# A fused attention and gated MLP kernel whose hand-ordered step list is reordered behind chunk 0's first layer

## The chip, the core and the metric

The kernel runs on one core of a Trainium2 chip. Engines: TensorE (PE, with its weight loads PEld), VectorE (DVE), ScalarE (ACT), GpSimd (POOL), and SyncE (SP), which here issues DMAs only. The metric is the device time of one execution in microseconds (us); lower is better.

## The reference: what is computed

```python
# q, k, v: [8 batches, 8 heads, 576 tokens, 64]; w_in: [512, 2048]; w_out: [2048, 512]
# causal attention within a sliding window of 64 tokens
scores = q @ k^T, masked to 0 <= i - j < window
x = softmax(scores) @ v                 # -> [4608 tokens, 512]
h = x @ w_in                            # [4608, 2048]
g = h - tanh(h)
out = g @ w_out                         # [4608, 512]
```

## The kernel before, in words

The kernel is a sequence of steps that a person or a search wrote out beforehand. `PLAN` (L536 and following) is a string of words; `play` splits it, and each word calls one function of the table `STEPS` with its numbers (`H.2.5` is `first_layer(2, 5)`; a letter p, a, v or s at the end names the engine: GpSimd, ScalarE, VectorE or SyncE). Each engine and each DMA queue takes its instructions in the order in which the words stand; across engines, semaphores make a step wait for the steps it needs. Nothing reorders it afterwards, so the order of words is the order on every queue.

The MLP works on 9 chunks of 512 tokens (c = 0 to 8):
- `H.c.m` is one of 16 first-layer products of a chunk, four matmuls of 128x512 into one PSUM bank (L431); `Hp.c.m.h` is half of one (L508). Banks: m modulo 2 for c over 1, (m + c) modulo 3 before.
- `A.c.m` takes the tanh of it on ScalarE (L439), `G.c.m` subtracts on VectorE and writes gT (L445); that frees the bank for the next `H`.
- `W.c.s.part` is a quarter of a second-layer product for 128 tokens, four matmuls (L474; L467 for the last block), in bank 2 (chunk 0: 2 and 0; chunk 8: 0 and 2). `O.c.s.eng` copies the sum to ysb, of which there are three buffers (L90 on ScalarE, L92 on VectorE), and SyncE sends it out (L495).

The attention works on pairs of heads g (batch g // 4). For batches up to 2:
- `lk`, `lq` load k and q rows, `ck`, `cq` cast them to bf16; `Fp`, `Ep` transpose them on TensorE (L260) into the bank given as last number, `Fc`, `Ec` copy them out; `Rp` makes the scores (L286), `Rx` their exp (L318).

For batches 3 to 7:
- `lr`, `qr` load k and q rows on GpSimd (L166); `tk`, `tq` transpose them by DMA, issued on SyncE (L171 and L179); `tz` copies the tail of q into q8; `S` makes the scores (L299, L304), `Sx` their exp (L314).

For all pairs:
- `M` multiplies by the 0/1 mask (L323). The mask itself lies in PSUM, in columns 448 to 511 of bank 7. `PP` multiplies with v (L348, banks 5 to 7), `DR` takes the reciprocal of the row sums (L356), `DN` divides (L365, L368), and `Xp`/`Xc` on TensorE (L397) or `Y` by DMA (L416) transposes the result into the x of the MLP.
- `LV` loads v rows on GpSimd (L145), and `Z.b` copies the rows that two tiles share from one half of the partitions to the other, two VectorE copies (L151, L152); in batch 1 `za` and `zb` do this per pair on an engine that is named.
- `wo` loads a part of w_out (L198). `mk` clears two tiles of k by memset on VectorE (L222).

The code that plays the list:

```python
    def play(script):
        for word in script.split():
            what, *args = word.split(".")
            STEPS[what](*[ENG[a] if a in ENG else int(a) for a in args])
```

## Time and profile before

| | |
|---|---|
| time of three runs | 307.33, 307.46, 308.23 us (median 307.46) |
| span of the profiled execution, first to last instruction | 305.2 us |
| the profiled execution's own time | not listed; the median of the runs is 2.26 us longer than its span |
| PE, DVE, ACT, POOL busy | 297.8, 176.2, 157.5, 103.7 us |
| bytes moved by DMA | 36.77 MB, 120 GB/s on average |

In the lines below, a timeline row has the start in us, the busy time in us, engine, line, operation, tiles out<-in, shapes and a count; in brackets stands how long the engine was idle before it and which instruction ended that. Overlapping matmuls are grouped into one row. A groups row of the page has the busy total and the mean in ns of one instruction.

### The profile page before, as it was taken

The numbers are of one execution on the slowest core, as the hardware profiler recorded it, in microseconds if no ns is written. First come the engines' busy times: TensorE is split into PE (matmuls) and PEld (weight loads), VectorE is DVE, ScalarE is ACT, GpSimd is POOL, SyncE is SP. The second block draws the span as 40 slices with busy tenths as digits, with TensorE's granted clock in tenths as the row PEclk, the third lists the DMA queues.
The fourth block names the chain that finished last, engine by engine and source line by source line (L and its number), as shares of the span: only waits on it lengthen the run. The fifth ranks groups of instructions, "written<-read, shape, count | busy, mean of one in ns | idle before, by whom it ended". The sixth has DMA issues, their size and how long they took to land.

```text
span 305.2 us, 6469 instructions
## 1 busy us (share of the span) xinstructions
PE 297.8 (98%) x2599; PEld 149.4 (49%) x2632; DVE 176.2 (58%) x316; ACT 157.5 (52%) x265; POOL 103.7 (34%) x141
## 2 busy tenths in 40 slices
...
PEclk9999999999999999999999999999999999999999
...
GB/s 155 159 195 193 195 207 180 159 205 102 102 143 127 173 125 181 182 108 131 164 177 127 135 173 142 95 143 35 37 76 74 0 69 37 34 34 37 52 51 104
DMA packets 132878, 36.77 MB, mean 120 GB/s; under 512 B 119920, under 2 KB 127344, under 8 KB 132848
## 3 DMA queue, kind: packets, MB, share of 16 engines
...
q8 instruction: 20, 0.33, 0.5%
q14 instruction: 10, 0.08, 0.1%
HBM read 36.70 MB, written 9.44 MB: 151 GB/s over the span
## 4 chain that ended last, share of the span: by engine, by line
PE 87%; DVE 5%; ACT 3%; issue 2%; POOL 2%; DVEq 0%; ACTq 0%; POOLq 0%
PE ps L474 38%; PE ps L431 30%; PE ps L508 6%; PE ps L348 3%; PE ps L304 2%; DVE gT L445 2%; PE ps L397 1%; ACT th L439 1%; PE ps L286 1%; PE ps L467 1%; DVE pt L323 1%; PE ps L260 1%; PE ps L281 1%; PE ps L227 1%; POOL qall L110 1%
## 5 line engine op out<-in xcount | busy, mean ns | idle before, releaser
L445 DVE TENSOR_TENSOR gT<-ps,th 128x512 bf16<-128x512 f32 x144 | 97.2, 687 | 85.3 <-ACT th L439 84.6
L474 PE MATMUL ps<-w_out_sb,gT 128*128 128x512 bf16 x527 | 131.5, 380 | 2.2 <-issue 0.8
L439 ACT ACTIVATE th<-ps 128x512 f32<-128x512 f32 x144 | 84.7, 599 | 93.0 <-PE ps L431 79.7
L431 PE MATMUL ps<-xT,wi 128*128 128x512 bf16 x496 | 120.7, 380 | 0.1
L474 PEld LDWEIGHTS <-gT 128*128 128x128 bf16 x560 | 53.3, 98 | 61.4
L431 PEld LDWEIGHTS <-wi 128*128 128x128 bf16 x496 | 47.0, 98 | 54.3
L145 POOL DMA_DIRECT2D vw<-in_v_dram x35 | 30.0, 872 | 36.1 <-PE ps L348 33.5
L90 ACT ACTIVATE ysb<-ps 128x512 f32<-128x512 f32 (+1 forms) x24 | 14.2, 593 | 30.9 <-PE ps L474 30.2
L166 POOL DMA_DIRECT2D qall<-in_q_dram x25 | 21.7, 881 | 24.1 <-DMA qw<-qall 21.4
L166 POOL DMA_DIRECT2D kall<-in_k_dram x25 | 21.7, 875 | 10.4 <-DMA kw<-kall 4.8
L314 ACT ACTIVATE pt<-ps 128x1024 bf16<-128x1024 f32 (+1 forms) x30 | 23.3, 816 | 3.5 <-PE ps L304 3.2
L323 DVE TENSOR_TENSOR pt<-pt,ps 128x1152 bf16<-128x1152 bf16 x28 | 20.5, 749 | 5.1 <-ACT pt L314 3.2
L508 PE MATMUL ps<-xT,wi 128*128 128x512 bf16 x80 | 20.8, 380 | 0.0
L92 DVE COPY ysb<-ps 128x512 f32<-128x512 f32 (+1 forms) x11 | 7.1, 650 | 20.5 <-PE ps L467 13.2
L368 DVE TENSOR_TENSOR xs<-ps,rcp 128x384 bf16<-128x384 f32 x28 | 15.2, 550 | 0.3
L318 ACT ACTIVATE pt<-ps 128x640 bf16<-128x640 f32 (+1 forms) x24 | 14.7, 659 | 0.8 <-PE ps L286 0.8
L348 PEld LDWEIGHTS <-pt 128*64 128x64 bf16 x504 | 9.4, 112 | 6.3 <-DVE pt L323 2.1
L90 ACT ACTIVATE kt<-ps 128x576 bf16<-128x576 bf16 x10 | 6.5, 647 | 10.8 <-PE ps L256 6.8
L227 PE MATMUL ps<-warm 128*128 128x512 bf16 (+1 forms) x35 | 10.6, 435 | 1.1 <-DVE warm L207 1.1
L508 PEld LDWEIGHTS <-wi 128*128 128x128 bf16 x80 | 7.4, 98 | 8.5 <-issue 0.4
L348 PE MATMUL ps<-vw,pt 128*64 128x65 bf16 x504 | 11.0, 197 | 0.3 <-DVE pt L323 0.2
L365 DVE TENSOR_TENSOR xs<-ps,rcp 128x384 bf16<-128x384 f32 x14 | 7.7, 550 | 0.1
...
## 6 DMA issues: line engine op xcount, KB each, us to landing
...
```

The costliest lines, as they stand in the source:

```text
L90: nc.scalar.activation(o, i, ACT.Copy)
L145: nc.gpsimd.dma_start(out=w[:, 2 * i + 1, :, 0:D] if i < NF else w[64:128, 2 * i, :, 0:D], in_=v[b, :, 128 * i:128 * i + n].rearrange("h p ...
L166: nc.gpsimd.dma_start(out=token_rows(b, n)[0:c, i], in_=(q if n == "q" else k)[b, :, 128 * i:128 * i + c].rearrange("h p d -> p h d"))
L314: nc.scalar.activation(o, sp, ACT.Exp, scale=scale)
L323: nc.vector.tensor_tensor(p, p, mask.unsqueeze(1).to_broadcast([128, 2 * NJ, 64]), ALU.mult)
L348: nc.tensor.matmul(ps[r, bank, 65 * i:65 * i + 65], PT[(g + r2) % NPT][:, j, r], vw[b % 2][:, j, p0 + r2 + NP * h, :], start=True, stop=True)
L368: nc.vector.tensor_tensor(xs[b % 2][:, p0 // 2, 0:6, n // 2, :], ov[:, :, 0:D], sums[g][:, n].to_broadcast([128, 6, D]), ALU.mult)
L431: nc.tensor.matmul(hp, w_in_tile(ki, m), chunk_tile(c)[:, n.start // 64:n.stop // 64, ki % 2, 64 * (ki // 2):64 * (ki // 2) + 64], start=( ...
L439: nc.scalar.activation(th[:, n], hp, ACT.Tanh)
L445: nc.vector.tensor_tensor(gT[c][:, m, columns(s)], hp, th, ALU.subtract)
L474: nc.tensor.matmul(yp, gT[c][:, m, s * 128:(s + 1) * 128], w_out_sb[:, m, :], start=n == 1 and i == 0, stop=n == 4 and i == 3)
L508: nc.tensor.matmul(hp, w_in_tile(half + 2 * i, m), chunk_tile(c)[:, :, half, 64 * i:64 * i + 64], start=n == 1 and i == 0, stop=n == 2 and ...
```

## The change

Only the string `PLAN` changes. Up to `cq.8.v G.0.9 G.0.10 Rp.7.1.3 A.0.11 wo.2 Fc.8.7.a G.0.11 Rp.7.0.5 H.0.12 lk.9.p Rx.7.0.5 A.0.12` (about 36 us into the span) it is the same word by word; behind that the same steps stand in another order to the end. A few steps take another engine (some casts and copies `c`, `Xc`, `O`, `tz`) or another bank for a transpose or a score (`Ep.8` takes bank 7 in place of 1, `Ep.9` bank 1 in place of 7). The number of TensorE instructions is the same. In the new order GpSimd's loads and SyncE's transposes stand in batches of about ten, and `wo` is loaded in the order 2, 1, 3 in place of 2, 3, 1.

The first lines, and those around the places that the prediction speaks of:

```diff
-        cq.8.v G.0.9 G.0.10 Rp.7.1.3 A.0.11 wo.2 Fc.8.7.a G.0.11 Rp.7.0.5 H.0.12 lk.9.p Rx.7.0.5 A.0.12 Ep.8.1
-        Rx.7.1.3 cq.9.v H.0.14 M.4 wo.3 zb.1.3.p G.0.12 Ec.8.1.a PP.4 wo.1 A.0.14 H.0.15 mk DR.4 DN.4.1 G.0.14
-        A.0.15 H.0.13 DN.4.0 za.1.3.a W.0.0.0 Rp.8.0.3 G.0.15 A.0.13 Rp.8.1.5 DN.4.2 zb.1.2.a za.1.2.v Rx.8.1.5
-        W.0.1.0 M.7 qr.3.3 LV.2.3 lk.11.p PP.6 Rx.8.0.3 Xp.1.0.1.3 W.0.0.2 G.0.13 Xp.1.0.0.4 DR.6 Xc.1.0.1.3.a
...
-        A.1.3 Rx.10.1.3 H.1.4 A.1.4 G.1.3 Ec.11.6.a H.1.5 A.1.5 qr.3.0 Z.2 H.1.6 qr.3.2 PP.8 G.1.5 Rp.11.0.3
...
-        G.2.2 H.2.5 Sx.12.2 Sx.12.0 W.1.1.1 Z.3 W.1.1.0 A.2.5 Sx.12.1 O.1.1.a tk.4.1 tq.4.0 M.12 tk.4.0 H.2.4
-        M.13 tk.4.3 tq.4.4 G.2.5 A.2.4 PP.12 W.1.2.3 H.2.7 lr.6.4 lr.5.4 DR.12 DN.12.2 G.2.4 tq.4.3 tk.4.2
...
+        cq.8.v G.0.9 G.0.10 Rp.7.1.3 A.0.11 wo.2 Fc.8.7.a G.0.11 Rp.7.0.5 H.0.12 lk.9.p Rx.7.0.5 A.0.12 Ep.8.7
+        Rx.7.1.3 cq.9.v H.0.14 M.4 wo.1 H.0.13 Ec.8.7.a M.7 G.0.12 A.0.14 PP.4 Rp.8.1.3 H.0.15 A.0.13 Rx.8.1.3
+        G.0.14 DR.4 G.0.13 DN.4.2 DN.4.0 DN.4.1 Rp.8.0.3 zb.1.3.a wo.3 za.1.3.p zb.1.2.p Rx.8.0.3 A.0.15
+        za.1.2.v Ep.9.1 W.0.0.0 Xp.1.0.0.3 Xp.1.0.1.4 Xc.1.0.1.4.a Xc.1.0.0.3.a Ec.9.1.a ck.9.a G.0.15 PP.6
...
+        qr.4.1 LV.3.0 A.1.1 ck.10.v M.8 W.0.3.3 Fp.11.4 Fc.11.4.a Ep.10.6 Ec.10.6.a W.0.3.2 O.0.3.a A.1.3
+        Ec.11.5.v G.1.1 mk Z.2 G.1.3 H.1.4 Hp.1.2.0 Hp.1.2.1 A.1.4 A.1.2 Fp.10.3 Rp.11.0.5 Rp.11.1.4 Rx.11.0.5
+        Fc.10.3.a H.1.6 tk.3.1 tk.3.4 tq.3.4 tk.3.3 tq.3.0 tq.4.4 tq.3.2 tk.3.2 tq.3.3 tq.3.1 tk.3.0 G.1.2 G.1.4
+        M.9 H.1.5 A.1.6 Rx.11.1.4 H.1.7 PP.8 G.1.6 A.1.5 A.1.7 G.1.5 DR.8 DN.8.1 DN.8.2 H.1.9 H.1.8 A.1.9 G.1.7
+        G.1.9 A.1.8 DN.8.0 G.1.8 Rp.10.1.3 Rp.10.0.6 H.1.10 H.1.12 Rx.10.1.3 Rx.10.0.6 A.1.10 M.10 M.11 G.1.10
+        H.1.11 Xp.2.0.1.4 A.1.11 A.1.12 PP.10 H.1.13 G.1.11 A.1.13 tz.3.a DR.10 G.1.12 DN.10.0 G.1.13 DN.10.1
...
+        O.1.0.a Hp.2.1.1 Hp.2.1.0 W.1.1.3 W.1.1.1 A.2.1 A.2.0 lr.5.3 qr.4.2 LV.3.1 LV.4.0 lr.4.0 lr.4.1 lr.4.3
+        LV.3.4 lr.5.2 LV.4.2 qr.5.4 lr.4.4 qr.5.2 qr.4.3 G.2.1 G.2.0 H.2.5 H.2.2 S.12 A.2.5 A.2.2 Sx.12.1 G.2.5
+        G.2.2 H.2.7 W.1.1.2 W.1.1.0 A.2.7 Sx.12.0 Sx.12.2 O.1.1.a G.2.7 H.2.9 H.2.10 W.1.2.2 W.1.2.3 A.2.9
+        A.2.10 Z.3 M.12 G.2.9 M.13 PP.12 G.2.10 H.2.6 A.2.6 DR.12 G.2.6 DN.12.1 DN.12.0 DN.12.2 W.1.2.0 W.1.2.1
...
+        G.3.15 M.21 W.3.0.1 Hp.4.0.0 W.3.0.2 W.3.0.3 Hp.4.0.1 Hp.4.1.0 Hp.4.1.1 O.3.0.v Z.5 W.3.1.3 A.4.1 A.4.0
+        Sx.22.1 G.4.1 G.4.0 M.20 W.3.1.1 H.4.3 W.3.1.0 H.4.2 W.3.1.2 A.4.3 A.4.2 Sx.22.2 G.4.3 H.4.7 A.4.7
...
```

Of the kernel before, what the change touches and what calls it, by code (L numbers as in the profile page):

```python
# [15 lines left out]
def kernel(  # L16
# [515 lines left out]
    def play(script):  # L532
# [24 lines left out]
        DN.6.2 DN.6.0 W.0.1.2 DN.6.1 Xp.1.1.0.5 lk.10.p ck.9.a Xc.1.0.0.4.a Fp.9.3 Xc.1.1.0.5.a Xp.1.1.1.4
        lr.3.2 lq.10.p lq.11.p LV.2.2 Hp.1.0.0 Ep.9.7 Xc.1.1.1.4.v Ec.9.7.a Fc.9.3.a Hp.1.0.1 W.0.1.3 W.0.0.3
        qr.3.4 LV.2.0 Rp.9.1.5 Rp.9.0.3 LV.2.1 W.0.0.1 O.0.0.a M.8 LV.2.4 W.0.1.1 lr.3.1 lr.3.4 A.1.0 tq.3.4
        G.1.0 O.0.1.a Rx.9.1.5 Rx.9.0.3 ck.11.a M.9 ck.10.a W.0.2.1 W.0.2.0 W.0.2.3 W.0.2.2 W.0.3.2 qr.3.1  # L560
        O.0.2.a Fp.11.5 cq.10.v W.0.3.1 W.0.3.3 Hp.1.1.1 W.0.3.0 Fp.10.7 Ep.10.3 Hp.1.1.0 O.0.3.v Ec.10.3.v
# [5 lines left out]
        A.1.13 A.1.14 Xc.2.0.1.3.a PP.10 H.1.15 LV.4.1 LV.3.1 A.1.15 Xc.2.0.0.4.a LV.3.3 G.1.13 LV.3.2 LV.3.0
        DR.10 DN.10.1 DN.10.0 tk.3.0 DN.10.2 tk.3.3 LV.3.4 LV.4.0 G.1.14 lr.4.2 qr.4.0 lr.4.1 lr.4.0 qr.5.3
        LV.4.2 W.1.0.1 W.1.0.2 Xp.2.1.1.6 W.1.0.0 G.1.15 qr.4.1 lr.4.4 Xp.2.1.0.5 Xc.2.1.0.5.a W.1.0.3
        Xc.2.1.1.6.v qr.4.3 lr.4.3 H.2.3 Hp.2.0.0 Hp.2.0.1 tk.4.4 O.1.0.a A.2.3 LV.4.3 qr.4.4 LV.4.4 A.2.0  # L570
        W.1.1.2 G.2.3 Hp.2.1.0 tz.3.a Hp.2.1.1 W.1.1.3 G.2.0 qr.4.2 qr.5.4 lr.5.2 H.2.2 A.2.1 G.2.1 S.12 A.2.2
# [5 lines left out]
        Xp.3.0.0.4 W.1.3.2 G.2.11 tq.5.4 W.1.3.3 H.2.12 A.2.12 H.2.13 Z.4 A.2.13 W.1.3.1 G.2.12 G.2.13 H.2.14
        W.1.3.0 H.2.15 DN.14.2 O.1.3.a DN.14.1 A.2.15 A.2.14 DN.14.0 Xp.3.1.0.6 W.2.0.1 Xp.3.1.1.7 W.2.0.0
        G.2.14 W.2.0.2 Xc.3.1.1.7.v Xc.3.0.0.4.a Xc.3.1.0.6.a G.2.15 qr.5.0 Hp.3.0.0 W.2.0.3 Hp.3.1.1 Hp.3.1.0
        O.2.0.a A.3.1 W.2.1.1 Hp.3.0.1 W.2.1.2 G.3.1 tz.4.v A.3.0 S.16 Sx.16.2 W.2.1.3 Sx.16.1 G.3.0 H.3.3  # L580
        W.2.1.0 M.17 Sx.16.0 M.16 H.3.2 A.3.3 PP.16 G.3.3 O.2.1.a A.3.2 tk.5.2 qr.5.1 qr.6.4 H.3.5 LV.5.3
        W.2.2.1 DR.16 A.3.5 tk.5.1 DN.16.2 tq.5.2 G.3.2 DN.16.1 H.3.4 DN.16.0 Y.4.0 A.3.4 S.18 G.3.5 W.2.2.0
        H.3.7 G.3.4 Sx.18.1 A.3.7 Sx.18.2 G.3.7 W.2.2.3 H.3.6 A.3.6 Sx.18.0 tk.6.4 tk.5.3 tq.5.0 tq.5.1 H.3.9
        tk.5.0 M.19 W.2.2.2 G.3.6 qr.7.1 H.3.8 M.18 A.3.9 PP.18 A.3.8 O.2.2.v G.3.9 DR.18 G.3.8 DN.18.2 DN.18.1
        DN.18.0 W.2.3.0 W.2.3.3 H.3.11 qr.6.2 lr.6.0 LV.5.4 lr.6.2 LV.5.0 A.3.11 W.2.3.1 G.3.11 Y.4.1 tq.6.4
        H.3.10 W.2.3.2 A.3.10 tq.6.2 G.3.10 O.2.3.a H.3.13 H.3.14 A.3.13 LV.5.1 LV.5.2 lr.6.1 qr.6.1 A.3.14
        G.3.13 W.3.0.2 H.3.15 tz.5.v G.3.14 qr.6.3 H.3.12 W.3.0.0 A.3.15 G.3.15 Hp.4.1.0 A.3.12 G.3.12 Hp.4.1.1
        A.4.1 W.3.0.1 G.4.1 W.3.0.3 Hp.4.0.1 H.4.3 Hp.4.0.0 O.3.0.v tk.6.3 tk.6.2 A.4.0 S.20 A.4.3 Sx.20.2
        Sx.20.0 Sx.20.1 tq.6.0 tk.6.0 W.3.1.1 G.4.0 G.4.3 W.3.1.0 H.4.2 W.3.1.3 A.4.2 S.22 G.4.2 H.4.4 W.3.1.2
        H.4.7 A.4.4 G.4.4 M.20 O.3.1.a Sx.22.0 Sx.22.1 A.4.7 W.3.2.1 H.4.6 W.3.2.2 A.4.6 Sx.22.2 W.3.2.3 Z.5  # L590
        G.4.7 M.22 M.21 H.4.9 PP.20 G.4.6 tq.7.1 tq.6.1 A.4.9 tk.6.1 tq.6.3 W.3.2.0 O.3.2.a DR.20 DN.20.2 G.4.9
        DN.20.0 DN.20.1 H.4.8 A.4.8 tz.6.a W.3.3.3 H.4.5 M.23 PP.22 A.4.5 G.4.8 DR.22 G.4.5 LV.7.1 W.3.3.0
        H.4.10 Y.5.0 DN.22.2 H.4.11 DN.22.1 W.3.3.2 A.4.11 A.4.10 DN.22.0 W.3.3.1 G.4.11 H.4.13 S.24 Y.5.1
        LV.6.1 LV.6.4 O.3.3.a G.4.10 H.4.12 A.4.13 LV.6.3 W.4.0.0 Sx.24.2 G.4.13 Sx.24.0 A.4.12 LV.6.2 G.4.12
        H.4.15 W.4.0.1 H.4.14 A.4.15 W.4.0.2 lr.7.2 G.4.15 Hp.5.1.0 LV.6.0 qr.7.3 LV.7.2 Hp.5.1.1 A.4.14 G.4.14
        qr.7.0 lr.7.1 Sx.24.1 Hp.5.0.1 Hp.5.0.0 qr.7.2 A.5.1 M.25 W.4.0.3 lr.7.3 G.5.1 O.4.0.a A.5.0 qr.7.4
        H.5.3 A.5.3 W.4.1.0 G.5.0 W.4.1.3 H.5.2 M.24 A.5.2 Z.6 G.5.3 W.4.1.2 W.4.1.1 G.5.2 O.4.1.a PP.24 H.5.5
        lr.7.0 lr.7.4 LV.7.0 LV.7.4 LV.7.3 tq.7.3 A.5.5 H.5.4 DR.24 A.5.4 DN.24.0 G.5.5 W.4.2.3 G.5.4 DN.24.2
        H.5.7 DN.24.1 H.5.6 S.26 A.5.6 W.4.2.0 Sx.26.0 A.5.7 Y.6.0 tq.7.4 tk.7.4 G.5.6 H.5.8 W.4.2.1 G.5.7
        W.4.2.2 H.5.9 A.5.8 Sx.26.2 M.26 tk.7.1 tk.7.0 tk.7.2 Sx.26.1 G.5.8 tq.7.0 A.5.9 H.5.10 O.4.2.v W.4.3.0  # L600
        tk.7.3 W.4.3.1 G.5.9 tq.7.2 H.5.11 A.5.10 A.5.11 M.27 G.5.11 PP.26 DR.26 W.4.3.3 W.4.3.2 DN.26.2 G.5.10
        DN.26.1 DN.26.0 O.4.3.a H.5.13 H.5.12 tz.7.v A.5.13 W.5.0.1 A.5.12 G.5.13 G.5.12 H.5.15 Y.6.1 H.5.14
        W.5.0.0 W.5.0.2 A.5.14 A.5.15 S.28 G.5.14 G.5.15 W.5.0.3 Hp.6.1.0 Hp.6.1.1 Hp.6.0.0 O.5.0.v W.5.1.1
        Sx.28.2 Sx.28.1 A.6.1 G.6.1 Hp.6.0.1 Sx.28.0 M.28 M.29 A.6.0 H.6.3 W.5.1.2 G.6.0 W.5.1.3 A.6.3 H.6.2
        G.6.3 Z.7 A.6.2 G.6.2 H.6.5 PP.28 H.6.4 A.6.5 W.5.1.0 G.6.5 H.6.7 A.6.4 DR.28 O.5.1.a DN.28.0 G.6.4
        A.6.7 H.6.6 DN.28.2 DN.28.1 S.30 Sx.30.0 A.6.6 G.6.7 W.5.2.1 H.6.9 Sx.30.1 W.5.2.2 A.6.9 G.6.6 Sx.30.2
        H.6.8 W.5.2.0 W.5.2.3 G.6.9 M.31 A.6.8 O.5.2.a M.30 H.6.11 G.6.8 Y.7.0 H.6.10 PP.30 A.6.11 G.6.11 A.6.10
        G.6.10 W.5.3.0 H.6.13 H.6.12 DR.30 DN.30.1 DN.30.2 DN.30.0 Y.7.1 A.6.12 A.6.13 G.6.12 W.5.3.1 W.5.3.2
        W.5.3.3 H.6.14 G.6.13 O.5.3.a H.6.15 W.6.0.1 W.6.0.0 W.6.0.2 A.6.14 A.6.15 G.6.15 G.6.14 Hp.7.0.1
        Hp.7.0.0 A.7.0 Hp.7.1.0 Hp.7.1.1 W.6.0.3 G.7.0 H.7.6 A.7.1 A.7.6 G.7.1 H.7.3 O.6.0.v G.7.6 A.7.3 W.6.1.3  # L610
        H.7.4 G.7.3 H.7.7 A.7.4 A.7.7 W.6.1.1 W.6.1.2 G.7.4 G.7.7 H.7.9 A.7.9 G.7.9 H.7.8 W.6.1.0 H.7.5 A.7.8
        A.7.5 G.7.8 O.6.1.v H.7.2 W.6.2.1 A.7.2 G.7.2 W.6.2.3 G.7.5 H.7.12 H.7.11 W.6.2.0 W.6.2.2 A.7.11 A.7.12
        G.7.11 G.7.12 O.6.2.v H.7.13 H.7.10 A.7.13 A.7.10 W.6.3.1 W.6.3.2 G.7.10 H.7.14 G.7.13 W.6.3.0 A.7.14
        H.7.15 G.7.14 A.7.15 W.6.3.3 Hp.8.0.0 Hp.8.0.1 G.7.15 Hp.8.1.0 O.6.3.a W.7.0.0 Hp.8.1.1 W.7.0.3 A.8.1
        W.7.0.2 A.8.0 G.8.1 G.8.0 H.8.7 H.8.2 A.8.7 A.8.2 W.7.0.1 G.8.7 G.8.2 H.8.3 H.8.4 A.8.4 A.8.3 O.7.0.v
        W.7.1.1 G.8.4 W.7.1.2 G.8.3 H.8.6 H.8.5 A.8.6 G.8.6 A.8.5 W.7.1.0 H.8.10 A.8.10 G.8.5 G.8.10 W.7.1.3
# [34 lines left out]
```

More of the change, by code (lines that the diff above doesn't have):

```diff
@@ L557 @@
[L557 to L561, printed above, removed]
@@ L567 @@
[L567 to L571, printed above, removed]
@@ L577 @@
[L577 to L616, printed above, removed]
@@ new lines @@
+        Rx.7.1.3 cq.9.v H.0.14 M.4 wo.1 H.0.13 Ec.8.7.a M.7 G.0.12 A.0.14 PP.4 Rp.8.1.3 H.0.15 A.0.13 Rx.8.1.3
+        G.0.14 DR.4 G.0.13 DN.4.2 DN.4.0 DN.4.1 Rp.8.0.3 zb.1.3.a wo.3 za.1.3.p zb.1.2.p Rx.8.0.3 A.0.15
+        za.1.2.v Ep.9.1 W.0.0.0 Xp.1.0.0.3 Xp.1.0.1.4 Xc.1.0.1.4.a Xc.1.0.0.3.a Ec.9.1.a ck.9.a G.0.15 PP.6
+        W.0.1.0 W.0.1.2 Hp.1.0.0 DR.6 DN.6.0 DN.6.2 DN.6.1 Xp.1.1.1.4 Xc.1.1.1.4.v Xp.1.1.0.6 Xc.1.1.0.6.a
+        W.0.0.2 Fp.9.3 Hp.1.0.1 W.0.0.1 W.0.1.1 W.0.0.3 W.0.1.3 lk.11.p LV.2.2 lq.10.p lq.11.p LV.2.4 LV.2.1
@@ new lines @@
+        lk.10.p LV.2.3 O.0.1.v O.0.0.a Fc.9.3.a W.0.2.1 W.0.2.2 LV.2.0 qr.3.0 lr.3.1 lr.3.4 qr.4.0 cq.10.a A.1.0
+        qr.4.4 qr.3.3 qr.3.4 lr.3.3 qr.3.1 W.0.3.1 cq.11.v ck.11.v Ep.11.5 W.0.2.0 Rp.9.1.6 Rp.9.0.3 G.1.0
+        W.0.2.3 Rx.9.0.3 O.0.2.a Rx.9.1.6 H.1.3 W.0.3.0 Hp.1.1.0 Hp.1.1.1 LV.3.3 qr.3.2 lr.3.2 lr.3.0 LV.3.2
+        qr.4.1 LV.3.0 A.1.1 ck.10.v M.8 W.0.3.3 Fp.11.4 Fc.11.4.a Ep.10.6 Ec.10.6.a W.0.3.2 O.0.3.a A.1.3
+        Ec.11.5.v G.1.1 mk Z.2 G.1.3 H.1.4 Hp.1.2.0 Hp.1.2.1 A.1.4 A.1.2 Fp.10.3 Rp.11.0.5 Rp.11.1.4 Rx.11.0.5
@@ new lines @@
+        Fc.10.3.a H.1.6 tk.3.1 tk.3.4 tq.3.4 tk.3.3 tq.3.0 tq.4.4 tq.3.2 tk.3.2 tq.3.3 tq.3.1 tk.3.0 G.1.2 G.1.4
+        M.9 H.1.5 A.1.6 Rx.11.1.4 H.1.7 PP.8 G.1.6 A.1.5 A.1.7 G.1.5 DR.8 DN.8.1 DN.8.2 H.1.9 H.1.8 A.1.9 G.1.7
+        G.1.9 A.1.8 DN.8.0 G.1.8 Rp.10.1.3 Rp.10.0.6 H.1.10 H.1.12 Rx.10.1.3 Rx.10.0.6 A.1.10 M.10 M.11 G.1.10
+        H.1.11 Xp.2.0.1.4 A.1.11 A.1.12 PP.10 H.1.13 G.1.11 A.1.13 tz.3.a DR.10 G.1.12 DN.10.0 G.1.13 DN.10.1
+        DN.10.2 H.1.14 Xp.2.0.0.3 H.1.15 Xc.2.0.0.3.v A.1.14 A.1.15 W.1.0.0 Xp.2.1.0.6 Xp.2.1.1.7 W.1.0.1
@@ new lines @@
+        Xc.2.1.0.6.a Xc.2.0.1.4.v G.1.15 G.1.14 Xc.2.1.1.7.a H.2.3 Hp.2.0.1 W.1.0.2 Hp.2.0.0 A.2.3 G.2.3 W.1.0.3
+        O.1.0.a Hp.2.1.1 Hp.2.1.0 W.1.1.3 W.1.1.1 A.2.1 A.2.0 lr.5.3 qr.4.2 LV.3.1 LV.4.0 lr.4.0 lr.4.1 lr.4.3
+        LV.3.4 lr.5.2 LV.4.2 qr.5.4 lr.4.4 qr.5.2 qr.4.3 G.2.1 G.2.0 H.2.5 H.2.2 S.12 A.2.5 A.2.2 Sx.12.1 G.2.5
+        G.2.2 H.2.7 W.1.1.2 W.1.1.0 A.2.7 Sx.12.0 Sx.12.2 O.1.1.a G.2.7 H.2.9 H.2.10 W.1.2.2 W.1.2.3 A.2.9
+        A.2.10 Z.3 M.12 G.2.9 M.13 PP.12 G.2.10 H.2.6 A.2.6 DR.12 G.2.6 DN.12.1 DN.12.0 DN.12.2 W.1.2.0 W.1.2.1
@@ new lines @@
+        H.2.4 A.2.4 G.2.4 lr.4.2 qr.5.1 LV.4.1 tq.4.1 tq.4.0 tk.4.1 tk.4.0 tk.4.3 tq.4.2 tk.4.2 tk.4.4 tq.4.3
+        O.1.2.a H.2.11 S.14 W.1.3.2 W.1.3.1 W.1.3.3 A.2.11 Sx.14.0 Sx.14.1 Sx.14.2 tz.4.v M.15 M.14 G.2.11
+        Xp.3.0.0.4 Xp.3.0.1.3 H.2.8 A.2.8 PP.14 DR.14 DN.14.1 G.2.8 H.2.13 A.2.13 W.1.3.0 O.1.3.a H.2.12 A.2.12
+        G.2.13 G.2.12 DN.14.2 DN.14.0 H.2.15 W.2.0.2 H.2.14 W.2.0.0 W.2.0.1 Xp.3.1.1.6 Xp.3.1.0.5 LV.4.3 lr.6.1
+        lr.6.0 LV.4.4 qr.6.2 lr.5.4 qr.6.0 lr.5.1 qr.5.0 LV.5.0 tk.5.4 tk.5.3 tk.5.2 tq.5.0 tq.5.4 tq.5.1 tq.5.2
```

51 lines of the change are left out of this document (40 added, 11 removed).

## The prediction
> **What bounds the kernel now.** I read the page first, then the busy table by windows, then the timeline around every gap of TensorE.
>
> ```profile
> span 305.2 us, 6469 instructions
> ...
> PE 297.8 (98%) x2599; PEld 149.4 (49%) x2632; DVE 176.2 (58%) x316; ACT 157.5 (52%) x265; POOL 103.7 (34%) x141
> ...
> PEclk9999999999999999999999999999999999999999
> ```
>
> TensorE is busy for 98% of the span, and in each of the 40 slices its granted clock (PEclk) has the highest digit. The words of the plan up to `G.0.11 ... A.0.12` are the same in both kernels, so the stretch in question begins at about 36 us. The windows view has its bounds, length, then the busy time and instructions of PE, PEld, DVE, ACT and POOL:
>
> ```profile
> 36.00:301.00 265.00, 262.43 (x2130) 129.62 (x2161) 152.86 (x259) 130.48 (x220) 71.94 (x88) 1.00 1.15 113
> ```
>
> Of 265.00 us TensorE is busy 262.43. The multiplications are the same ones after the change, so it can only win out of what is idle, and part of that are the turns from one kind of matmul to another, which both orders make about equally often. Waits that a reorder can remove are the following; I found four places.
>
> First, chunk 0's end, where masks and PV products of pairs 4 to 7 run between the first-layer products (`H`, L431):
>
> ```profile
> 37.38 0.42 PE L260 MATMUL ps<-ident,qb 96*128 96x96 bf16 x6
> 37.64 1.03 PE L431 MATMUL ps<-xT,wi 128*128 128x512 bf16 x4
> 37.90 0.73 DVE L323 TENSOR_TENSOR pt<-pt,ps 128x1152 bf16<-128x1152 bf16 x1
> 38.56 0.69 ACT L90 ACTIVATE qp<-ps 128x576 bf16<-128x576 bf16 x1
> 38.56 0.68 DVE L445 TENSOR_TENSOR gT<-ps,th 128x512 bf16<-128x512 f32 x1
> 38.69 0.76 PE L348 MATMUL ps<-vw,pt 128*64 128x65 bf16 x36
> ...
> 39.38 1.90 PE L431 MATMUL ps<-xT,wi 128*128 128x512 bf16 x8
> 39.49 0.27 DVE L356 RECIPROCAL rcp<-ps 128x18 f32<-128x18 f32 x1
> 39.80 0.56 DVE L365 TENSOR_TENSOR xs<-ps,rcp 128x384 bf16<-128x384 f32 x1
> ```
> ```profile
> 42.45 1.04 PE L474 MATMUL ps<-w_out_sb,gT 128*128 128x512 bf16 x4
> 43.54 0.91 PE L348 MATMUL ps<-vw,pt 128*64 128x65 bf16 x36
> ```
> ```profile
> 99.63 0.59 PE L431 MATMUL ps<-xT,wi 128*128 128x512 bf16 x2
> 100.16 0.77 PE L348 MATMUL ps<-vw,pt 128*64 128x65 bf16 x36
> ```
>
> Four matmuls are busy 1.03 and eight 1.90, so one of 512 columns comes every 0.217 us, and four are 0.87. At 99.63, where nothing waits, two of them and the turn to a PV product take 0.53: the turn costs 0.09. From 37.64 to `PP.4` at 38.69 are 1.05, where 0.87 + 0.09 = 0.96 would do: 0.09 late, behind its mask `M.4` (37.90 + 0.73 = 38.63, then 0.05 to the matmul). `PP.6` (43.54) starts 1.09 behind 42.45, 0.13 late, and takes 0.91 where the undisturbed ones take 0.76: 0.28 in all.
>
> Second, the rows of v that lie across two tiles are copied by `Z` (L151, L152):
>
> ```profile
> 64.81 1.24 PE L431 MATMUL ps<-xT,wi 128*128 128x512 bf16 x5
> 66.11 0.76 PE L348 MATMUL ps<-vw,pt 128*64 128x65 bf16 x36
> ```
> ```profile
> 64.66 0.70 DVE L151 COPY vw<-vw 64x2080 bf16<-64x2080 bf16 x1
> 65.36 0.70 DVE L152 COPY vw<-vw 64x2080 bf16<-64x2080 bf16 x1
> ```
>
> Five matmuls from 64.81 and the turn end at 65.98; `PP.8` starts at 66.11, 0.05 behind the copy's end: 0.13 lost. Third and fourth, the same in batch 3:
>
> ```profile
> 87.31 1.22 DVE L151 COPY vw<-vw 64x2080 bf16<-64x2080 bf16 x1
> 88.56 0.74 DVE L152 COPY vw<-vw 64x2080 bf16<-64x2080 bf16 x1
> 89.33 1.42 DVE L323 TENSOR_TENSOR pt<-pt,ps 128x1152 bf16<-128x1152 bf16 x2
> ```
> ```profile
> 89.14 1.03 PE L431 MATMUL ps<-xT,wi 128*128 128x512 bf16 x4
> 90.14 0.47 PE L348 MATMUL ps<-vw,pt 128*64 128x65 bf16 x18
> 90.81 0.47 PE L348 MATMUL ps<-vw,pt 128*64 128x65 bf16 x18 [0.19 <-DVE pt L323]
> ```
> ```profile
> 87.02 0.99 POOL L166 DMA_DIRECT2D qall<-in_q_dram  x1
> 87.89 0.92 POOL L166 DMA_DIRECT2D kall<-in_k_dram  x1
> ```
>
> Here the two copies take 1.96 instead of 1.40, with GpSimd issuing DMAs beside them, and both masks come late: 36 products take 0.76 and 18 take 0.47, so 18 follow each other in 0.30, so 90.81 is 0.37 late, and 90.14 is 0.05 late. I count 0.09 + 0.28 + 0.13 + 0.42 = 0.92 us in all. That is the most the new order can gain here; what follows `W.8.3` keeps its length, since the last three evictions have the same sizes and the last copy has 2 us of matmuls in front of it.
>
> **What the change removes, moves and adds.** It moves instructions on all queues and adds none. All four waits are gone in the new order: the steps that caused them stand elsewhere (`Z.2` far ahead of `PP.8`, `zb` and `za` ahead of `PP.6`, another neighbour for `M.4`). What is late next I found by walking the new order with the durations of these rows, each queue in its order. A first-layer product must wait for the subtraction `G` that frees its bank: `G` has 0.68 alone and about 0.61 in a row, as its successor starts before its end (38.56 behind 37.90 + 0.73); 0.05 lies between DVE and the matmul.
>
> 1. `PP.4`, second half, +0.31. Its mask `M.7` reads the mask kept in bank 7, and `Ep.8` now transposes into bank 7, so `M.7` waits until `Ec.8` has emptied it: 38.56 + 0.69 = 39.25, + 0.03 + 0.75 + 0.05 = 40.08. TensorE comes from `H.0.14` (37.64) and `H.0.13`: 8 x 0.217 + 0.09 = 39.47, and 18 products (0.30): 39.77. The difference is 0.31. That a mask waits for such an emptying stands in the old trace also, where a pair is emptied from bank 7:
>
> ```profile
> 48.96 0.76 DVE L323 TENSOR_TENSOR pt<-pt,ps 128x1152 bf16<-128x1152 bf16 x1 [0.75 <-ACT qp L90]
> ```
>
> The Trainium skill, page "PSUM — Partial Sum Buffer", section "PSUM bank collisions raise a hardware error", asks for a guard by bank and quadrant, not by address; it speaks against this edit, since the reading of the mask columns and the emptying of other columns may not overlap. The row agrees (0.75 us of waiting). If the columns could be read side by side, this term would be nothing and the sum 0.31 less.
>
> 2. `Ep.9`, +0.17. It goes into bank 1, which `G.0.13` frees; that now stands behind `M.7`, `G.0.12`, `G.0.14` and `DR.4`: 40.03 + 0.61 + 0.61 + 0.27 + 0.61 = 42.13, less some 0.08 that `G.0.12` starts ahead of the mask's end, and 0.05 to the matmul: 42.10. TensorE has 40.08 + 0.42 for the products and the turn, and some 1.43 for two score steps (0.2 to 0.3 each) with `H.0.15` (0.87) between: 41.93.
>
> 3. `PP.6` behind the copy `za.1.2.v` and the next `W.0` behind `G.0.15`: 0.10 + 0.08. `PP.8` behind exp into bank 7, which in turn waits for `M.9`: 0.08. A chunk 1 product behind a `G` that stands behind `DR.8` and two norms (0.27 + 0.56 + 0.56): 0.17. These four are estimates from the same sums, each good to 0.1.
>
> 4. `Z.5` at about 147 us now stands on DVE between `O.3.0.v` and `G.4.1`, which `H.4.3` waits for. From the last matmul of `W.3.0`: 0.42 + 0.69 (the copy out of PSUM, next row) + 1.40 + 0.69 + 0.05 = 3.25 and about 0.1 of handovers; TensorE has 15 matmuls, 3.25. So +0.1 with undisturbed copies (0.13 by the walk). GpSimd issues loads about then.
>
> ```profile
> 130.56 0.69 DVE L92 COPY ysb<-ps 128x512 f32<-128x512 f32 x1
> ```
> ```profile
> 179.67 1.03 DVE L151 COPY vw<-vw 64x2080 bf16<-64x2080 bf16 x1
> 180.71 0.81 DVE L152 COPY vw<-vw 64x2080 bf16<-64x2080 bf16 x1
> ```
> ```profile
> 179.32 2.68 POOL L145 DMA_DIRECT2D vw<-in_v_dram  x3 [0.33 <-DMA vw<-in_v_dram]
> ```
>
> With issues beside it the pair of copies took 1.84 or 1.96, so 0.44 to 0.56 more; `Z.5` has one or two issues near it, and I take +0.30, that is 0.43 in all (ends 0.1 and 0.7).
>
> 5. `Z.3` at about 90 us: the batch of thirteen loads runs on GpSimd at the time. With 0.56 more the masks `M.12`, `M.13` and the `G` behind them are late by what their slack (about 0.25) does not cover: +0.31; undisturbed 0, since then both have their slack. Nearest row 87.31, which has just this neighbourhood, so I take 0.31.
>
> The Trainium skill, page "SBUF — State Buffer", section "Who interferes with whom", says that VectorE copies in a two-port mode and GpSimd hold one port pair exclusively, and the second blocks entirely. The trace agrees in kind (0.70 against 1.22 and 1.03), not in size: an issue there is 0.92 to 0.99 and no copy lost over 0.52. It is weighed as rival (d).
>
> 6. Small waits of up to 0.05 for second-layer banks: about 0.35 in the new order against 0.26 in the old one, +0.09. The batches of loads on GpSimd and of transposes on SyncE cost nothing as long as they land in time (below). `mk` is two memsets ahead of `Z.2`, with room.
>
> Sum of new waits: 0.31 + 0.17 + 0.18 + 0.08 + 0.17 + 0.43 + 0.31 + 0.09 = 1.74; less 0.92: +0.82. The profiled execution's span of 305.2 becomes 306.0. Its own time is not listed; the median of the runs, 307.46, lies 2.26 above its span, and I add to the median: 308.28, rounded 308.3. About 0.3%, 0.92 us, is what a measurement of this kernel can tell from no change: 306.54 to 308.38 counts as the same.
>
> **Rivals.** (a) The copies are not disturbed: 4 falls to 0.13 and 5 to 0: +0.21, 307.7. Against: the old kernel's copies with issues beside them were slow both times; for it: issues can fall a microsecond off.
>
> (b) Slower: late landings. The new order issues loads and transposes in batches, and waits in ACT's queue for one of them: `tz.3.a`, behind `A.1.13`, copies from the third of eleven transposes that are issued behind the out-DMA of `O.0.3.a`. The first answer is on L179 (transposes of q), the second on L166 (loads of q and k):
>
> ```profile
> DMA to landing us min/median/max: 2.3/4.8/8.2
> ```
> ```profile
> DMA to landing us min/median/max: 3.7/6.7/12.6
> ```
>
> From the end of `W.0.3` to the need: ten whole and two half `H` (9.5), two `PP` (1.6), scores and transposes (1.4), waits (0.4) and a tanh (1.0): 13.9. To its issue: eviction 1.0, out-DMA 0.9, two transposes 2.4: 4.3. It decides from a landing of 9.6 us on; 8.2 is the longest of before, but its source is a load that can take 12.6. Behind it wait the tanh of all later products, so every us late is one us: 1 to 2.6, 309.3 to 310.9, likeliest 309.3. Against: the median has 5 us to spare. `tz.5.a` and the casts of pair 10 are like it, with 3 and 1 us.
>
> (c) The waits of my walk are covered (a mask or a `G` earlier than I count) and only the gain stays: 307.46 - 0.92 = 306.54. Against: 1 and 2 follow from few rows.
>
> (d) A copy that meets an issue loses all of it, 0.9: `Z.5` then costs 0.13 + 0.9 in place of 0.43 and `Z.3` 0.9 - 0.25 in place of 0.31: 0.94 more, 309.2. Against: 0.52 was the most of three disturbed copies. This is what the page on SBUF would give.
>
> **How the numbers follow.** The sum holds with 0.46: 308.0 to 308.8, half on each side of 308.38. Rival (a) 0.18, same. Rival (b) 0.26 and (d) 0.04, slower. Rival (c) 0.06, counted as faster with orders that gain still more. Same 0.23 + 0.18 = 0.41, slower 0.23 + 0.26 + 0.04 = 0.53, faster 0.06. The range leaves out (c) and the upper part of (b): 307.3 to 309.8.
>
> **What would show it.** In the new trace: `PP.4`'s second half near 40.1 behind DVE L323; a gap of 0.1 to 0.6 behind DVE L445 near 149; `Z` copies over 1 us near 90 and 147; the gaps at 43.5, 66.0 and 90.8 gone; TensorE busy 262.4 in a stretch of about 265.8. Gaps behind ACT L90 into `q8` near 76 or 127 us show (b). A wait longer than 0.6 us anywhere, or none at 40.1, shows the prediction wrong.

## The result, and the profile after

The new order takes 309.5 us (median of 6 runs, 308.49 to 309.79); the kernel before, run beside it, 307.61 (307.26 to 308.23). The ratio is 1.0048 (95% interval 1.0031 to 1.0065; ratios here are taken over all runs, so they need not equal that of the two medians): slower by 0.5%, inside the range and on the side that had the larger chance, but 1.2 us above the time forecast. The profiled execution took 309.69 us with a span of 308.0, 2.8 more than the span before. In five of the runs further down the granted clock was 0.993 to 0.995 where it was 0.998 to 1.000 in all others, and these five are the longest of all (310.4 to 312.3 us).

A transfer is called issued when its instruction starts on its queue, and landed when its semaphore tells that it is complete. The page of the changed kernel has these first lines, DMA row of the slices, chain that ended last and group of part 5 (busy total, mean ns, then the idle time just before it and what ended that):

```profile
span 308.0 us, 6504 instructions
...
PE 300.5 (98%) x2632; PEld 149.8 (49%) x2632; DVE 178.2 (58%) x319; ACT 154.8 (50%) x260; POOL 105.9 (34%) x143
...
DMA  9999999999999999999999992331014011000112
...
PE 57%; DMA 22%; POOL 11%; issue 4%; DVE 3%; SPq 2%; ACT 0%; POOLq 0%
...
L508 PE MATMUL ps<-xT,wi 128*128 128x512 bf16 x80 | 21.0, 379 | 2.0 <-DMA xT<-xs 2.0
```

The DMA row of the kernel before:

```profile
DMA  9999999995999999949999999560143010001112
```

TensorE's busy time cannot be set against that of before directly, since 33 records of L474 are missing there (527 of 560). The chain and the last row are the finding: DMA has entered the chain, and half a first-layer product (L508) stood 2.0 us idle for one transposition of x. (The 22% is how much of the chain runs through transfers, not time that was lost: a second trace of this kernel has 3% there, with half the idle time.) The DMA engines are now full without a break to slice 24 (185 us); before they had dips and ran on to slice 27.

The place in the timeline of TensorE, the queues of SyncE and GpSimd ahead of it, and the piece of the chain (start, duration, what):

```profile
175.48 0.59 PE L508 MATMUL ps<-xT,wi 128*128 128x512 bf16 x2
175.91 1.03 PE L474 MATMUL ps<-w_out_sb,gT 128*128 128x512 bf16 x4
178.93 1.45 PE L508 MATMUL ps<-xT,wi 128*128 128x512 bf16 x6 [1.99 <-DMA xT<-xs]
```
```profile
164.16 2.54 SPq L416 DMA_TRANSPOSE xT<-xs  x2
166.79 1.29 SPq L171 DMA_TRANSPOSE kw<-kall  x1
168.18 0.53 SPq L495 DMA_DIRECT2D out_dram<-ysb  x1
168.80 3.48 SPq L416 DMA_TRANSPOSE xT<-xs  x2
```
```profile
164.55 1.75 POOL L166 DMA_DIRECT2D qall<-in_q_dram  x2
166.28 3.33 POOL L145 DMA_DIRECT2D vw<-in_v_dram  x4
169.56 0.93 POOL L166 DMA_DIRECT2D kall<-in_k_dram  x1
170.43 0.93 POOL L145 DMA_DIRECT2D vw<-in_v_dram  x1
```
```profile
168.80 10.09 DMA xT<-xs
```

The four second-layer matmuls from 175.91 end their slot at 176.78; `Hp.5.0.1` starts at 178.93: 2.15 us lost, the largest single loss of the kernel behind its start. It needs the second half of chunk 5's x, which `Y.5.1` transposes. That was issued at 168.80 and landed 10.09 us later, with eight loads for batch 7 going out on GpSimd from 164.55 on. In the kernel before, the same transposition was issued at 165.55 and landed 7.63 us later, at 173.18; it was needed at 174.80, by the third of the eight matmuls below (SyncE, GpSimd, TensorE):

```profile
165.55 2.53 SPq L416 DMA_TRANSPOSE xT<-xs  x2
163.41 4.18 POOL L145 DMA_DIRECT2D vw<-in_v_dram  x5 [18.06 <-PE ps L348]
174.37 1.89 PE L508 MATMUL ps<-xT,wi 128*128 128x512 bf16 x8
```

So a slow landing is nothing new. Before had 9.25 us from issue to need, and 1.6 to spare; the new order leaves 7.98, and the landing takes 2.46 more.

The other places, in the order of the prediction's terms. `PP.4` (TensorE, then ScalarE's emptying and VectorE's mask):

```profile
38.38 1.89 PE L431 MATMUL ps<-xT,wi 128*128 128x512 bf16 x8
40.20 0.47 PE L348 MATMUL ps<-vw,pt 128*64 128x65 bf16 x18
40.93 0.47 PE L348 MATMUL ps<-vw,pt 128*64 128x65 bf16 x18 [0.25 <-DVE pt L323]
```
```profile
39.44 0.65 ACT L90 ACTIVATE qp<-ps 128x576 bf16<-128x576 bf16 x1
...
40.12 0.75 DVE L323 TENSOR_TENSOR pt<-pt,ps 128x1152 bf16<-128x1152 bf16 x1 [0.72 <-ACT qp L90]
```

18 products take 0.30, so the second half, 0.73 behind the first, is 0.43 late behind the mask, which waited 0.72 for the emptying of bank 7. (All of this is 0.74 later than in the trace before: `H.0.14` starts at 38.38 where it had 37.64. The words up to there are the same, and `H.0.14` starts anywhere from 37.72 to 38.75 in the other traces with these words, at 37.90 in a second trace of this kernel; so that is mostly the run and not the change.) `Z.5` with the `H.4.3` behind it, and `Z.3`:

```profile
147.32 0.70 DVE L151 COPY vw<-vw 64x2080 bf16<-64x2080 bf16 x1
148.03 0.97 DVE L152 COPY vw<-vw 64x2080 bf16<-64x2080 bf16 x1
```
```profile
147.69 1.89 PE L474 MATMUL ps<-w_out_sb,gT 128*128 128x512 bf16 x8
149.78 1.02 PE L431 MATMUL ps<-xT,wi 128*128 128x512 bf16 x4 [0.19 <-DVE gT L445]
```
```profile
90.77 0.98 DVE L151 COPY vw<-vw 64x2080 bf16<-64x2080 bf16 x1
91.78 0.95 DVE L152 COPY vw<-vw 64x2080 bf16<-64x2080 bf16 x1
```

Eight matmuls from 147.69 end their slot at 149.42; the product starts at 149.78, 0.36 late. Behind `Z.3`, near 95, the trace has the products of `PP.12` 0.05 late in their middle and `H.2.6` behind them 0.19.

### The profile page after: what moved, and what is told of

Its sections match the earlier page's. It is cut to its first block, busy times and chain, and to the rows that moved or that the text cites. A ratio compares the mean times of both kernels' runs of the same rounds, so it can differ in the third digit from the quotient of the medians.

```text
span 308.0 us, 6504 instructions
## 1 busy us (share of the span) xinstructions
PE 300.5 (98%) x2632; PEld 149.8 (49%) x2632; DVE 178.2 (58%) x319; ACT 154.8 (50%) x260; POOL 105.9 (34%) x143
## 4 chain that ended last, share of the span: by engine, by line
PE 57%; DMA 22%; POOL 11%; issue 4%; DVE 3%; SPq 2%; ACT 0%; POOLq 0%
PE ps L474 27%; PE ps L431 23%; DMA vw<-in_v_dram 8%; DMA qall<-in_q_dram 6%; DMA xT<-xs 3%; PE ps L508 3%; POOL vw L145 3%; DMA kw<-kall 2%; DMA wi<-in_moe_w_in_dram 2%; POOL kall L166 2%; PE ps L348 2%; POOL qall L166 2%; POOL qall L110 1%; PE ps L304 1%; PE ps L467 1%
## 5 line engine op out<-in xcount | busy, mean ns | idle before, releaser
L474 PE MATMUL ps<-w_out_sb,gT 128*128 128x512 bf16 x560 | 135.0, 379 | 0.0
L474 PEld LDWEIGHTS <-gT 128*128 128x128 bf16 x560 | 54.1, 98 | 63.6
L166 POOL DMA_DIRECT2D kall<-in_k_dram x25 | 22.4, 904 | 18.5 <-DMA kw<-kall 17.5
L90 ACT ACTIVATE ysb<-ps 128x512 f32<-128x512 f32 (+1 forms) x22 | 13.0, 592 | 27.0 <-PE ps L474 14.4
L508 PE MATMUL ps<-xT,wi 128*128 128x512 bf16 x80 | 21.0, 379 | 2.0 <-DMA xT<-xs 2.0
L92 DVE COPY ysb<-ps 128x512 f32<-128x512 f32 (+1 forms) x13 | 8.6, 660 | 21.5 <-PE ps L474 20.0
L368 DVE TENSOR_TENSOR xs<-ps,rcp 128x384 bf16<-128x384 f32 x28 | 14.7, 549 | 0.2
L508 PEld LDWEIGHTS <-wi 128*128 128x128 bf16 x80 | 7.3, 98 | 10.8 <-issue 2.7
L110 POOL DMA_DIRECT2D kall<-in_k_dram x11 | 7.2, 661 | 2.3 <-POOLq L635 0.9
```

Source lines behind the costliest of these rows:

```text
L90: nc.scalar.activation(o, i, ACT.Copy)
L166: nc.gpsimd.dma_start(out=token_rows(b, n)[0:c, i], in_=(q if n == "q" else k)[b, :, 128 * i:128 * i + c].rearrange("h p d -> p h d"))
L474: nc.tensor.matmul(yp, gT[c][:, m, s * 128:(s + 1) * 128], w_out_sb[:, m, :], start=n == 1 and i == 0, stop=n == 4 and i == 3)
L508: nc.tensor.matmul(hp, w_in_tile(half + 2 * i, m), chunk_tile(c)[:, :, half, 64 * i:64 * i + 64], start=n == 1 and i == 0, stop=n == 2 and ...
```

## The experiments

Each is the new order with the words moved that its diff shows. What is called the landing of `Y.5.1` is that of its first transposition, the one for chunk 5; the second is for chunk 6.

**e1_gate: the loads behind the transposition.**

```diff
-  tk.6.2 tq.7.4 tq.6.3
+  tk.6.2 tq.6.3
-  LV.6.0 tz.7.p qr.7.1 qr.7.0 LV.7.1 LV.7.0 LV.7.3 LV.7.4 lr.7.2 LV.7.2 Y.5.1
+  Y.5.1 tq.7.4 LV.6.0 tz.7.p qr.7.1 qr.7.0 LV.7.1 LV.7.0 LV.7.3 LV.7.4 lr.7.2 LV.7.2
```

> The new order with one transposition (tq.7.4) and with it the batch of nine loads that waits for it on GpSimd (tz.7.p and behind) put behind Y.5.1. In the new kernel's trace TensorE waits 1.99 us (176.94 to 178.93) for Y.5.1, the transposition of chunk 5's x, which was issued at 168.80 and landed 10.09 us later, with the nine loads issued from 164.55 on. Theory (the transposition queues behind loads that nobody needs yet): it lands in 2.3 to 3.5 us, the gap of 2.15 us is gone, the time falls by 1 to 2.2 us to 307.4, and the spread of the runs with it. Rival (its place on SyncE's queue, behind tk.7.3 and an out-DMA): only the 1.2 us of one issue are won, a gap of about 0.9 stays. Rival (a run's accident): nothing changes.

307.32 us median of 12 runs (before beside it 307.87), ratio 0.998 (0.9966 to 0.9994). TensorE, SyncE and GpSimd:

```profile
175.53 1.03 PE L474 MATMUL ps<-w_out_sb,gT 128*128 128x512 bf16 x4
176.40 1.46 PE L508 MATMUL ps<-xT,wi 128*128 128x512 bf16 x6
```
```profile
166.91 2.53 SPq L416 DMA_TRANSPOSE xT<-xs  x2
```
```profile
173.33 1.75 POOL L166 DMA_DIRECT2D qall<-in_q_dram  x2
```

The loads begin at 173.33, the transposition lands in 2.3 us, and the product follows with no gap (0.87 behind four matmuls). The late landing was the loss; without it the new order is not slower than the kernel before but 0.2% faster. The loads held back are eight: `LV.6.0`, the ninth word that moved, goes out at 147 to 148 us in both orders. The edit takes one transposition out of SyncE's way too, so it does not tell loads from place; the next two were to do that. In this trace `Z.5`'s copies took 1.07 and 0.97, and the gap at 149 grew to 0.73.

**e2_early: some of the loads earlier, SyncE's queue untouched.**

```diff
-  LV.6.0 tz.7.p qr.7.1 qr.7.0 LV.7.1 LV.7.0 LV.7.3 LV.7.4 lr.7.2 LV.7.2 Y.5.1
+  LV.6.0 qr.7.1 qr.7.0 lr.7.2 LV.7.1 LV.7.0 LV.7.3 LV.7.4 LV.7.2 Y.5.1
-  O.3.3.v G.4.14
+  O.3.3.v G.4.14 tz.7.a
```

> The new order with tz.7 moved from GpSimd to ScalarE and behind O.3.3, so that four of the nine loads (LV.6.0, qr.7.1, qr.7.0, lr.7.2) no longer wait on GpSimd for tq.7.4 and go out from about 150 us on; the other five wait for PP.22 as before. SyncE's order is untouched. Theory of the loads: sixteen transfers landed in 17 us behind 164.2, so four fewer ahead are about 4 us: Y.5.1 lands near 174.8, before it is needed at 176.8, the gap is gone, time about 307.5. Rival of SyncE's place: Y.5.1 is issued as before, and the gap of 2.15 us stays.

308.29 us median of 12 runs, ratio 1.0007 (0.9993 to 1.0022). The chain and TensorE:

```profile
169.89 7.79 DMA xT<-xs
```
```profile
176.61 1.03 PE L474 MATMUL ps<-w_out_sb,gT 128*128 128x512 bf16 x4
177.72 1.46 PE L508 MATMUL ps<-xT,wi 128*128 128x512 bf16 x6
```

The gap falls from 2.15 to 0.25 with SyncE's order as it was, so the loads have a large part in the lateness. The time shows less of it: 308.29 lies between the 307.32 of e1_gate and the 309.36 of e3_bank below, which has the loads in their old place; all three ran beside the same runs of the kernel before. And the reckoning was wrong. Three loads went out earlier and not four, two of q and one of k, since `LV.6.0` had not waited before. The five that are left, all of v, go out ahead of the transposition as five did before (two of q, three of v), so as many transfers stand in front. What is missing is the three loads issued just behind it. The landing took 7.79 us, where the four traces with the loads in their old place have 9.02 to 10.09. In a single line served in the order of issue, what is issued behind would make no difference. In two lines that take turns it could: the Trainium skill, page "DMA: Bandwidth & Descriptors", section "Queues, rings and completion order", says that each DMA engine goes round its queue rows packet by packet. The 1.2 to 2.3 us agree with it; no run here shows the turns themselves, and none separates them from the other difference, that v loads stand in front in place of q loads.

**e2_order: one transposition out of the way, loads untouched.**

```diff
-  Y.5.0 tk.7.3 H.4.9
+  Y.5.0 H.4.9
-  lr.7.2 LV.7.2 Y.5.1
+  lr.7.2 LV.7.2 Y.5.1 tk.7.3
```

> The new order with tk.7.3 alone put behind Y.5.1 on SyncE's queue; the loads are untouched. Theory of the loads: one of some sixteen transfers is taken from ahead of it (1.07 us each), a gap of 0.9 to 1.2 us stays, time about 308.5. Rival of SyncE's place: the issue comes 1.3 us earlier and the transfer with it takes its usual 3.7 us, no gap, time 307.4.

307.68 us median of 12 runs, ratio 0.9982 (0.9966 to 0.9999): as good as the first, where the theory of the loads had left a gap of about 1.

```profile
167.28 3.44 SPq L416 DMA_TRANSPOSE xT<-xs  x2
```
```profile
175.99 1.03 PE L474 MATMUL ps<-w_out_sb,gT 128*128 128x512 bf16 x4
176.85 1.46 PE L508 MATMUL ps<-xT,wi 128*128 128x512 bf16 x6
```

Neither theory was right as written. The transposition still took 8.73 us (it landed at 176.01), so the loads still held it and it did not come down to its usual 3.7; but it was issued 1.52 earlier and landed 2.87 earlier, 0.84 before it was needed. Reckoned from the landing of `Y.5.0` (167.61 and 167.35) that is 2.61 earlier; against the three other traces with the old place (a1_after, e3_bank, e5_z5), where it lies 10.15 to 10.40 behind that landing and here 8.66, it is 1.5 to 1.7. My 1.07 for one transfer fewer (1.17, since fifteen and not sixteen landed in 17.5 us) forgot that an earlier issue also puts one load behind it that was in front: four loads stand ahead here and not five. Two fewer would be 2.1 to 2.3, within the 1.5 to 2.6 of these traces.

**e3_bank: `Ep.8` in bank 3.**

```diff
-  Ep.8.7 ... Ec.8.7.a
+  Ep.8.3 ... Ec.8.3.a
```

> The new order with Ep.8 in bank 3 in place of bank 7. Theory (the mask M.7 waits for the emptying of its own bank): the 0.44 us gap of TensorE before the second half of PP.4 at 40.9 and the 0.03 of Ep.9 at 42.8 are gone, 0.1 to 0.2 come back at PP.6 and W.0.1 near 44; net 0.3 us less, 309.2 with the late landing unchanged. Rival (the mask itself is late): the gap stays at 0.4.

309.36 us median of 12 runs, ratio 1.0044 (1.0022 to 1.0066). The runs lie between 307.64 and 311.06, so the time cannot tell 0.3 us here; the trace, which has a gap of 1.49 us at the late landing, can:

```profile
38.62 1.89 PE L431 MATMUL ps<-xT,wi 128*128 128x512 bf16 x8
40.43 0.76 PE L348 MATMUL ps<-vw,pt 128*64 128x65 bf16 x36
```

All 36 products run through in 0.76; the wait of 0.43 was the bank. The 0.03 of `Ep.9` is gone as well, and nothing came back at `PP.6` in this trace.

**a1_after: the new order once more, e5_z5: `Z.5` alone moved** (beside the same runs of the kernel before as e4_best).

> The changed kernel again, beside the next two on one chip. If the late landing of Y.5.1 is a property of the order, the wait of TensorE before Hp.5.1 near 177 us is there again, 1.5 to 2.2 us, and the median lies 1.3 to 2 us above the kernel before. If it was an accident of the one profiled execution, there is no gap and the trace should then have some other loss of that size.

```diff
-  O.3.0.v Z.5 W.3.1.3 A.4.1 A.4.0 Sx.22.1 G.4.1 G.4.0 M.20
+  O.3.0.v W.3.1.3 A.4.1 A.4.0 Sx.22.1 G.4.1 G.4.0 Z.5 M.20
```

> The new order with Z.5 alone moved behind G.4.0. Theory: the gap before H.4.3 near 149 us (0.36) goes, the masks M.20 and M.21 behind the copies keep their room; Y.5.1 is late as before or later, since what stands behind starts 0.36 earlier while the loads do not: the gap at 177 is 2.1 to 2.5 us and the end gains nothing to 0.3 us. Rival (the late landing moves along with TensorE): the whole 0.36 us is gained.

The repeat: 308.54 us median of 9 runs, ratio 1.0057 (1.0028 to 1.0087) to 307.81 of before. The moved `Z.5`: 308.73, ratio 1.002 (1.0003 to 1.0036). The chain of the repeat, then of e5_z5:

```profile
168.17 9.09 DMA xT<-xs
```
```profile
167.75 9.02 DMA xT<-xs
```

The late landing is there each time, so it is no accident of one execution; but the gaps, 1.14 and 1.24 us, are smaller than either expectation said, and the repeat's median is only 0.7 above that of before. Both profiled executions are short ones: 308.09 is the least of the repeat's nine, and 307.59 belongs to four runs of e5_z5 at 307.0 to 307.6, while the other eight took 308.7 to 309.6. In e5_z5 the gap at 149 is gone (the six traces with `Z.5` in its new-order place have 0.35 to 0.73 there), and the transposition is issued 0.42 and lands 0.49 earlier than in the repeat: it moved along, so the rival of that expectation is nearer to the trace. The medians of the two do not show the gain.

**e4_best: the three edits of e1_gate, e3_bank and e5_z5 together.**

> The new order with three edits: Y.5.1 ahead of tq.7.4 and the nine loads behind it, Ep.8 in bank 3 in place of 7, and Z.5 behind G.4.0 in place of ahead of W.3.1.3. Theory: no gap at 177 (2.15 less than the profiled execution of the new kernel), none at 40.9 (0.47 less), none at 149 (0.36 to 0.73 less); what stays are 0.05 near 67, 0.15 near 70 and up to 0.24 near 95. About 0.8 us below the first experiment, 306.5 where that has 307.3, and 1.2 to 1.4 us below the kernel before on the same chip. Rival (one of the gaps comes back at the next wait): at most half of the 0.8 us is seen.

306.1 us median of 5 runs (306.02 to 306.49) against 307.81, ratio 0.995 (0.9936 to 0.9964): by the ratio 1.5 us faster than the kernel before, by the medians 1.7, a little more than was expected. The spread is the narrowest of all, of the fewest runs. Page, and TensorE near 175:

```profile
span 304.8 us, 6471 instructions
...
PE 96%; DVE 2%; issue 1%; ACT 1%
```
```profile
174.85 1.03 PE L474 MATMUL ps<-w_out_sb,gT 128*128 128x512 bf16 x4
175.72 1.46 PE L508 MATMUL ps<-xT,wi 128*128 128x512 bf16 x6
```

No DMA is left in the chain, which is 96% TensorE. Behind 38 us there remain gaps of 0.04 near 65 and 0.15 near 70.

## Why the prediction was right or wrong

The time lay in the range, and slower had the larger chance, but both came out by luck. The sum made the new order slower by reordering alone, with every transfer in time. What made it slower is a transfer that was not in time, at a place that the prediction did not name; with that out of the way (e1_gate) the new order is 0.5 us faster than the kernel before. That rival (b)'s 309.3 is so near to 309.5 is luck as well, since its price was that of another transfer.

| step | forecast | profiled execution |
|---|---|---|
| 1 `PP.4` behind `M.7` | +0.31 | +0.43 |
| 2 `Ep.9` behind `G.0.13` | +0.17 | +0.03 |
| 3 `PP.6` and `W.0`; `PP.8`; `H.1.10` | +0.18; +0.08; +0.17 | 0; +0.05; +0.15 |
| 4 `Z.5` | +0.43 | +0.36 |
| 5 `Z.3` | +0.31 | +0.24 |
| 6 small ones | +0.09 | none over 0.03 |
| the four waits of before | -0.92 | all gone, -0.92 |
| sum of the reorder | +0.82 | +0.34 |
| late landing, rival (b) | 0 | +2.15 |
| start, same words in both | 0 | +0.74 |

The measured ones come to 3.23; the last matmul starts at 304.92 in place of 301.67, 3.25 later, and the end behind it is 0.5 shorter in this execution. The 2.15 is the largest of four traces, which have 1.14, 1.24, 1.49 and 2.15. And the table compares with a short execution: the 35 runs of the kernel before that stand beside e1_gate have spans of 305.2 to 307.8, median 305.9, and times 1.6 to 2.0 above their spans. So the 2.26 that the forecast added to the span was in part the distance of a short execution from the median, and what the longer ones of before lose is in no trace here. That may be why the table has +0.34 for the reorder where e1_gate's times have -0.5; it stays open.

**The walk along the queues held, place by place.** Every wait over 0.1 us behind 36 us that VectorE or ScalarE causes in the new trace was named beforehand, with its place and its releaser. Term 1 was short because the emptying stood 1.06 behind the start of `H.0.14` and not 0.92. Term 2 and the first two of term 3 were differences of two long sums, each good to 0.1 at best. The first of term 3 comes and goes: `PP.6` and the `W.0` behind it lose nothing here, 0.36 and 0.10 in e2_early, 0.14 and 0.10 in e2_order, whose words are the same up to there.

**The copies.** Rivals (a) and (d) are both refuted: of the copies of 0.70 that meet an issue in the six traces, some kept their 0.70, the others took 0.81 to 1.18, and none lost 0.9. For `Z.5` the traces give the price: copies of 1.67, 1.78, 1.82 and 2.04 us together go with gaps of 0.36, 0.47, 0.51 and 0.73, the sum less 1.31 each time. Undisturbed copies of 1.40 would so cost 0.09. What decides whether a copy loses is when it starts within the issue. Two pairs, from e1_gate and from e5_z5:

```profile
90.60 0.88 POOL L145 DMA_DIRECT2D vw<-in_v_dram  x1 [0.44 <-PE ps L474]
90.83 1.15 DVE L152 COPY vw<-vw 64x2080 bf16<-64x2080 bf16 x1
```
```profile
90.00 1.33 POOL L145 DMA_DIRECT2D vw<-in_v_dram  x1
90.15 0.70 DVE L151 COPY vw<-vw 64x2080 bf16<-64x2080 bf16 x1
```

The first copy starts 0.23 into the issue, with 0.65 of it to come, and loses 0.45. The second starts 0.15 into it and loses nothing; there it is the issue that takes 1.33 in place of some 0.9. So it is in all nine traces: a copy that starts up to 0.19 into an issue loses nothing, and one that starts later, with more than 0.2 of it to come, loses what is left of the issue less about 0.2 (0.04 to 0.52 lost). The Trainium skill's rule (page "SBUF — State Buffer", section "Who interferes with whom"), that whoever issues first gets the shared ports for the whole instruction and the other blocks fully, agrees with this in that one of the two waits for the other; the copies do not lose the first and the last 0.2 us of an issue, and so less than the 0.9 of rival (d). The prediction's reading, that the trace does not bear out the size, took the whole issue where only its rest counts.

**The forecast failed at the landings.** It put the batches at nothing "as long as they land in time", and gave rival (b) 0.26. The mechanism of (b) was right, its place was not. `tz.3.a` was close: its transposition landed 8.58 us after its issue, and the copy ran at 76.43 without a wait, 0.86 behind the landing. The one that decided was `Y.5.1`, which the prediction did not name: its wait was put at nothing and measured 1.14 to 2.15 us. Its line L416 in the trace of before has this:

```profile
DMA to landing us min/median/max: 2.3/3.7/8.2
```

8.2 there is more than the 7.98 us that the new order leaves, and it is a landing of `Y.5.1` itself, of its second transposition. Had I set that row against each need, as I did for `tz.3.a`, the place could have been found, if the walk gave its 7.98 well enough. Setting one transfer against its need and not all was the error. The condition "from a landing of 9.6 us on" belongs to `tz.3.a`: the smallest distance of issue and need decides, and it lay here.

Why before escapes and the new order does not is two things together: the need comes 1.27 us sooner behind the issue, and the landing takes 2.46 more (1.4 to 1.7 in the three other traces), with five loads issued ahead of it since 164 where before had three since 163. e2_early and e2_order each show that a change to either queue alone takes away most of the gap in the trace; by the medians, against the 309.36 of e3_bank, e2_order gains nearly what e1_gate does and e2_early about half of it. Not settled is in what order the two queues are served.
